# A linear-attention block with an MLP on one core: the state product with its values stationary, a query-state product in four row parts, fixed PSUM places, and a new order of work

## The chip, the core and the metric

The kernel runs on one core of a Trainium2 chip. A core has a matrix engine (TensorE, in the profile PE, its weight loads PEld), a vector engine (VectorE, DVE), a scalar engine (ScalarE, ACT), a general engine (GpSimd, POOL) and a sync engine (SyncE, SP) that issues most transfers. Each engine works through its own instructions in order and waits on semaphores for the others. Matmuls write into PSUM, which here is eight banks of 512 fp32 values per partition; everything else lies in SBUF.

The metric is the time of one execution on the device in microseconds (us), median of several runs. Lower is better.

## What is computed

The input is one sequence of 2048 tokens of 640 features. First comes an attention block without a softmax over tokens: each of 32 heads (20 features each) maps queries and keys through a small matrix, takes a softmax over its 20 features of the result and of its negative, and uses these 40 numbers as positive features. Keys and values are summed over all tokens into a state of 40 x 20 a head, and each query reads the state. Then comes an MLP of width 1728. Both have a layer norm in front and a residual around them.

```python
def _A_ref(x, wqkv, w_phi, wo):
    ...
    pq = jnp.einsum("bhsd,hdf->bhsf", q, w_phi)
    pk = jnp.einsum("bhsd,hdf->bhsf", k, w_phi)
    phi_q = jnp.concatenate([_softmax(pq, axis=-1), _softmax(-pq, axis=-1)], axis=-1)
    phi_k = jnp.concatenate([_softmax(pk, axis=-1), _softmax(-pk, axis=-1)], axis=-1)
    kv = jnp.einsum("bhsf,bhsd->bhfd", phi_k, v)
    z  = jnp.einsum("bhsf->bhf", phi_k)
    num = jnp.einsum("bhqf,bhfd->bhqd", phi_q, kv)
    den = jnp.einsum("bhqf,bhf->bhq", phi_q, z)[..., None] + 1e-6
    o = num / den
    return (...)(o, 0, 2, 1, 3).reshape(B, S, D) @ wo
...
h = x + _A_ref(_layernorm(x, axis=-1), A_wqkv, A_w_phi, A_wo)
h2 = h + _B_ref(_layernorm(h, axis=-1), B_w1, B_w2)
```

## The kernel before

The 2048 tokens are 16 token tiles of 128 (t = 0 to 15), in four groups of four. The 640 features are five chunks of 128 (c or r). All operations are small functions op_xx, and a long string, ORDER, names them one by one with their arguments; the kernel walks through it, so each engine's instructions stand in the order of the string. The last letter of a word chooses an engine (a ACT, v VectorE, p POOL) or a queue (s SP).

The stages, with the words that the text below uses:

- Weights and input are loaded (lp, lk, lv, lx for w_phi, the key weights, the value weights and X; l1, l2, lo later). wt turns a chunk of the key weights (five transposes), wc copies it out, fk folds w_phi into it and fc copies the folded chunk Wfk. gk and gc do the same for the queries (lq loads these weights turned).
- For each tile, st takes the statistics on VectorE, rs the inverse deviation on POOL, xn normalizes, and either xt and xc (TensorE transposes and a copy) or xd (a transposing DMA) turn the tile. At the start VectorE fills a tile of zeros, and TensorE runs matmuls on it (wm, L255).
- vp and kp project values and keys: ten matmuls of 320 columns each. vc copies the values to Vp (32 heads of 20 values and a one, 21 columns), ke takes the exponential of plus and minus the keys on ACT, kr sums each head on VectorE, and ka divides on POOL (one of the 16 tiles is shared with VectorE, kb).
- cc, the **state product** (L407), adds a tile to the state in PSUM: for each sign s and each of ten slices of 64 key features one matmul, with 64 keys' columns as weights and four heads of Vp as 84 moving columns. The output's 64 partitions are the upper or lower half, so two matmuls stand side by side on the two column halves of the array. km multiplies the state by a mask, so that only a head's own block is left, into KVBD (bf16).
- qp projects queries (matmuls of 512 columns, five for each chunk of 128 features), qe takes the exponentials into EqT, with the features on partitions.
- dp, the **query-state product** (L460), runs once for each tile and sign: ten matmuls over 64 partitions (row halves), each of 88 columns (four heads of 22). dw then joins both signs: a reciprocal, a product of 32 columns, a product and an add of 672 columns on VectorE (L473 to L480). dr takes one more reciprocal, do divides on POOL or VectorE, td turns the tile by a transposing DMA.
- op multiplies by wo (ten matmuls of 320 columns), oa adds X on VectorE, sq, sa, sr and hn are the second layer norm, hd turns the tile.
- up is the MLP's first product (L596, and L606 for the last 64 rows), ua the silu on ACT, yp the second product (L642, and yh, L657, for the last 64 rows), yo adds the residual, so stores a tile.

PSUM is one pool of four buffers of two banks each. Every op_ function that needs one takes the next that comes free; the running state holds one of them for the whole key stage. The product of one tile takes two, one for each sign.

Of the kernel before, what the change touches and what calls it, by code (L numbers as in the profile page):

```python
# [9 lines left out]
ALU = mybir.AluOpType  # L10
# [18 lines left out]
lq.4 wc.4.v fc.3.a st.1 mo xt.2 kp.3.0.1 lq.0 xc.2.a kp.3.1.2 kp.3.2.3 st.0 fk.4 vp.2.0.3 fc.4.a  # L29
lx.8.12.s rs.0.2 lq.3 vp.3.3.5 kp.3.3.4 vc.3.a kp.3.4.5 xn.0.v vp.2.3.5 lq.1 xn.1.v ke.3 st.5  # L30
kp.2.0.1 kp.2.1.2 xt.0 lh.s kp.2.2.3 st.4 xc.0.a kp.2.3.4 xt.1 vc.2.a kp.2.4.5 lq.2 kp.0 st.6 rs.4.2
ke.2 xn.5.v vp.0 xc.1.a xn.4.v xd.5 st.7 ke.0 kp.1 st.11 lx.12.16.s rs.6.2 vc.0.a xd.4 st.8 vp.1
ke.1 xn.7.v st.10 gk.2 xd.7 gk.0 gc.2.a vp.5 st.9 vc.1.a lo.s gc.0.a kr.1 gk.3 rs.8.4 kp.5 gc.3.a
rm.10 gk.1 xn.9.v ke.5 ka.1.p vp.4 st.12 xd.9 gc.1.a st.14 kp.4 vc.5.a xn.8.v vc.4.a rm.6 st.15 xd.8
vp.7 ke.4 st.13 kp.7 xn.6.a kr.2 rs.12.4 xn.10.a xd.6 vp.9 ke.7 rm.13 xn.12.v ka.2.p kr.4 kp.9 xd.12
vc.9.a vc.7.a gk.4 l2.0.4.s ke.9 vp.8 xd.10 xn.14.v ka.4.p kr.0 gc.4.a vp.6 xn.13.a vc.8.a kr.3 kp.6
rm.11 rm.15 ka.0.p cc.2 kr.7 cc.1 ke.6 cc.4 kp.8 ka.3.p vc.6.a kr.5 xn.15.a qp.0.0 ke.8 xd.15 ka.7.p
kr.9 xd.14 vp.12 qe.0.0 l2.8.13.s ka.5.p kr.8 kp.12 l1.1.s vc.12.a xn.11.a qp.1.0 ke.12 ka.8.p xd.11
kr.12 kp.15 l1.0.s qe.1.0 xd.13 ka.9.p kp.10 l1.2.s l2.4.8.s cc.0 cc.7 ka.12.p ke.10 cc.3 cc.5 cc.8
kr.10 vp.10 kp.14 vc.10.a kr.6 ka.10.p ke.15 kp.11 ke.14 kp.13 ka.6.h ke.11 kr.14 vp.15 ke.13 kr.11  # L40
ka.14.p qp.0.2 qp.0.1 qe.0.2 kr.13 vc.15.a ka.11.p vp.13 kr.15 vp.14 ka.13.p vc.13.a qe.0.1 kb.6
vp.11 vc.14.v ka.15.p cc.12 vc.11.a cc.9 cc.6 cc.11 cc.10 cc.14 cc.13 cc.15 qp.1.2 km.0 close km.1
dp.1.0 qe.1.2 dp.1.1 qp.1.1 dw.1.v dp.0.1 qe.1.1 dp.0.0 dr.1 qp.2.1 dw.0.v dp.3.1 qe.2.1 dp.3.0 dr.0
qp.3.0 dw.3.v do.0.0.p do.0.1.p do.1.1.p td.0 dp.5.0 qe.3.0 dp.5.1 dr.3 qp.2.0 dw.5.v do.3.1.p
do.3.0.p do.1.0.p dp.4.1 td.1 qe.2.0 dp.4.0 op.0 dw.4.v td.3 qp.2.2 oa.0 dp.2.1 qe.2.2 dp.2.0 dr.5
sa.0 qp.3.2 dr.4 dw.2.v do.5.1.p sq.0 op.1 do.5.0.p qe.3.2 sr.0 td.5 dp.9.0 dp.9.1 dr.2 qp.3.1 hn.0
do.2.1.p do.2.0.v hd.0 oa.1 do.4.0.p do.4.1.p dw.9.v sq.1 td.2 op.3 sa.1 qe.3.1 sr.1 td.4 op.5 hn.1
dr.9 hd.1 op.2 oa.5 oa.3 sa.5 op.4 do.9.1.p oa.2 up.0.3 sq.2 oa.4 dp.10.1 sa.4 sq.4 dp.10.0 up.0.0
dw.10.v ua.0.3 sr.4 sq.5 sa.3 do.9.0.p dp.6.0 ua.0.0 dp.6.1 up.0.1 sa.2 dw.6.v td.9 sq.3 sr.3 dp.8.1
dr.10 ua.0.1 dp.8.0 sr.2 up.0.2 dw.8.v sr.5 do.10.0.p dp.7.0 do.10.1.v ua.0.2 dp.7.1 op.9 dr.6 hn.5  # L50
do.6.1.p hn.3 hd.5 do.6.0.p hn.2 yp.0.0 hn.4 hd.2 oa.9 yp.0.1 dw.7.v td.6 hd.3 yp.1.0 dr.8 do.8.0.v
hd.4 yh.0.0 dp.11.0 dp.11.1 yo.0 yp.1.1 do.8.1.v dr.7 dw.11.v do.7.1.p op.6 sa.9 up.1.0 do.7.0.v
# [12 lines left out]
ua.4.2 up.3.2 ua.3.4 yp.15.0 ua.3.2 up.3.5 yp.14.0 ua.3.5 yp.15.1 yp.10.0 yh.4.0 yh.3.0 yp.12.1
yp.12.0 yp.14.1 yo.12 so.12 yp.10.1 yp.11.1 yo.10 yo.14 yp.11.0 so.14 so.10 yh.3.1 yo.15 yq.13.0
yo.11 so.15 so.11 so.9 yq.13.1 yz.13.0 yz.13.1 sz.13.0.a sz.13.1.s
# [3 lines left out]
def kernel(  # L71
# [11 lines left out]
    nc = tc.nc  # L83
# [18 lines left out]
    HQ = [(64 * q) // DH for q in range(2 * C)]  # L102
# [8 lines left out]
    mm = ctx.enter_context(tc.tile_pool(name="mm", bufs=4, space=PSUM))  # L111

    def mm2():
        return mm.tile([P, 2, 512], F32, name="mm2")

    def mmT():
        return mm.tile([P, C, P], BF16, name="mm2")
# [14 lines left out]
    warm = first.tile([P, 512], BF16, name="warm")  # L132
    nc.vector.memset(warm[:], 0.0)
# [8 lines left out]
    maskS = persist.tile([P, C, 4, 1], BF16, name="maskS")  # L142
    KVBD = persist.tile([P, 2, C, 4, 22], BF16, name="KVBD")
# [58 lines left out]
    def op_mc():  # L202
        nc.gpsimd.memset(maskS[:], 1.0)
        d = 64 - DH * HQ[1]
        for lo in (0, 64):
            m = maskS[lo : lo + 64, :, :, 0]
            nc.gpsimd.affine_select(
                out=m, in_=m, compare_op=ALU.is_ge, fill=0.0,
                base=0, pattern=[[d, C], [-DH, 4]], channel_multiplier=1,
            )  # L210
            nc.gpsimd.affine_select(
                out=m, in_=m, compare_op=ALU.is_gt, fill=0.0,
                base=DH, pattern=[[-d, C], [DH, 4]], channel_multiplier=-1,
            )
        for s in range(2):
            nc.gpsimd.tensor_copy(KVBD[:, s, :, :, 21], maskS[:, :, :, 0])

# [35 lines left out]
    def op_wm(n=512, ps=None):  # L253
        ps = mm2() if ps is None else ps
        nc.tensor.matmul(ps[:, 0, 0:n], warm[:, 0:P], warm[:, 0:n], start=True, stop=True)  # L255
        return ps
# [78 lines left out]
    def op_gc(ce, eng="a"):  # L335
        copy(
            eng,
            Wfq[:, ce, :].rearrange("p (r a k) -> p a r k", r=C, a=2),
            tl["gk", ce][:, :, 0:320].rearrange("p a (r k) -> p a r k", r=C),
        )  # L340
# [54 lines left out]
    def op_cc(t):  # L395
        Ek, Vp = tl["ek", t], Vps[t % NV]
        if "kv" not in tl:
            kv = mm2()
            tl["kv"] = [kv[:, s, 0:420].rearrange("p (r j c) -> p r j c", r=C, j=4) for s in range(2)]
            tl["nkv"] = 0  # L400
        kv = tl["kv"]
        tl["nkv"] += 1
        for s in range(2):
            for r in range(C):
                for a in range(2):
                    q, lo = C * a + r, 64 * a
                    nc.tensor.matmul(  # L407
                        kv[s][lo : lo + 64, r, :, :].rearrange("p j c -> p (j c)"),
                        Ek[:, s, 64 * q : 64 * q + 64],
                        Vp[:, HQ[q] : HQ[q] + 4, :].rearrange("p h c -> p (h c)"),  # L410
                        start=(tl["nkv"] == 1 and r == 0),
                        stop=(tl["nkv"] == T),
                        skip_group_check=True,
                    )

    def op_km(s):
        nc.vector.tensor_tensor(
            KVBD[:, s, :, :, 0:21], tl["kv"][s], maskS[:].to_broadcast([P, C, 4, 21]), op=ALU.mult,
        )
# [34 lines left out]
    def op_dp(t, s):  # L454
        g, i = t // GT, t % GT
        ps = mm2()
        for r in range(C):
            for a in range(2):
                lo = 64 * a
                nc.tensor.matmul(  # L460
# [26 lines left out]
    def op_dr(t):  # L487
        rd = sm.tile([P, 2, 16], F32, name="rd")
        nc.vector.reciprocal(rd[:], tl["u", t][:, :, :, 20])  # L489
        tl["rd", t] = rd  # L490
# [228 lines left out]
```

## Time and profile before

| | us |
|---|---|
| median of 3 runs | 239.62 |
| range of the runs | 239.39 to 239.97 |
| the profiled execution, its own time | 240.42 |
| its span (first to last instruction) | 238.7 |
| VectorE, ACT, POOL busy | 136.3, 104.8, 88.8 |

The profile is one execution. A view that groups instructions gives busy time and the mean time of one; as matmuls overlap, a mean holds the latency, and the time that a matmul really takes is the distance between starts. The chain of waits is followed back from the last instruction: each piece is what the end depended on. In the timeline, the first number of a row is the start in us from the span's start, the second the length; a bracket gives the idle time of the engine before it and who ended it.

### The profile page before, as it was taken

How to read it: one execution, taken by the hardware profiler on the slowest of the kernel's cores; microseconds unless marked ns; L12 is line 12 of the kernel's file. 1: busy time of each engine (PE TensorE's matmuls, PEld its weight loads, DVE VectorE, ACT ScalarE, POOL GpSimd, SP SyncE). 2: the span in 40 equal slices, each digit the busy share in tenths (PEclk: the TensorE clock that was granted, in tenths of full speed). 3: DMA queues.
4: the chain of work that ended last, by engine and by line, in shares of the span. 5: the costliest groups of instructions: out<-in, count | busy, mean ns of one | idle time of the engine just before them, and what ended most of it. 6: DMA issues, size and time to landing. Idle time of an engine off the chain costs nothing.

```text
span 238.7 us, 5187 instructions
## 1 busy us (share of the span) xinstructions
PE 232.9 (98%) x2143; PEld 150.8 (63%) x2159; DVE 136.3 (57%) x256; ACT 104.8 (44%) x155; POOL 88.8 (37%) x166
## 2 busy tenths in 40 slices
PE   7999999999999999999999999999999999999994
PEld 3777777577584456787655476664566756656762
DVE  3779999938968999889858139623213120000133
ACT  3678897967545674561043620015660014631000
POOL 5722769998870737464101550001424000000000
PEclk9999999999999999999999999999999999999999
DMA  6997945499000136116480004520103701000013
GB/s 204 314 212 168 233 89 140 87 333 312 4 3 3 27 58 110 31 29 58 84 133 7 17 14 82 110 58 0 29 3 83 156 11 55 0 3 0 26 59 110
DMA packets 42807, 20.60 MB, mean 86 GB/s; under 512 B 34336, under 2 KB 42272, under 8 KB 42784
## 3 DMA queue, kind: packets, MB, share of 16 engines
q1 hardware_dynamic: 41984, 20.11, 36.8%
q8 instruction: 17, 0.28, 0.5%
q10 hardware_dynamic: 800, 0.16, 0.4%
q14 instruction: 6, 0.05, 0.1%
HBM read 9.61 MB, written 2.62 MB: 51 GB/s over the span
## 4 chain that ended last, share of the span: by engine, by line
PE 93%; DVE 2%; DMA 2%; issue 1%; ACT 1%; DVEq 0%
PE mm L596 24%; PE mm L642 21%; PE mm L348 18%; PE mm L427 9%; PE mm L522 9%; PE mm L460 3%; PE mm L407 3%; DMA out_dram<-ob 2%; PE mm L255 2%; PE mm L318 1%; PE mm L606 1%; PE mm L657 1%; ACT EqT L437 1%; PE mm L303 1%; DVE xn L278 1%
## 5 line engine op out<-in xcount | busy, mean ns | idle before, releaser
L618 ACT ACTIVATE shT<-mm 128x1024 bf16<-128x1024 f32 (+2 forms) x29 | 27.5, 963 | 77.9 <-PE mm L596 56.2
L596 PE MATMUL mm<-HnT,w 128*128 128x512 bf16 (+1 forms) x316 | 58.7, 335 | 0.5
L642 PE MATMUL mm<-w,shT 128*128 128x320 bf16 (+2 forms) x415 | 58.5, 299 | 0.2 <-issue 0.2
L642 PEld LDWEIGHTS <-shT 128*128 128x128 bf16 x416 | 39.8, 98 | 17.8 <-issue 1.3
L596 PEld LDWEIGHTS <-w 128*128 128x128 bf16 x325 | 31.2, 98 | 23.1 <-issue 0.4
L665 DVE TENSOR_TENSOR ob<-mm,X 128x640 bf16<-128x640 f32 x15 | 12.2, 822 | 46.7 <-PE mm L642 38.3
L348 PEld LDWEIGHTS <-XnT 128*128 128x128 bf16 x320 | 30.8, 98 | 12.3 <-DMA wv<-in_A_wqkv_dram 0.2
L385 POOL TENSOR_TENSOR Ek<-Ek,Sk 128x1280 bf16<-128x1280 bf16 (+1 forms) x16 | 36.9, 2332 | 2.5 <-DVE Sk L380 1.6
L377 DVE TENSOR_REDUCE Sk<-Ek 128x64 f32<-128x1280 bf16 x16 | 23.1, 1445 | 4.5 <-ACT Ek L369 4.5
L437 ACT ACTIVATE EqT<-mm 128x1024 bf16<-128x1024 f32 (+1 forms) x24 | 19.8, 879 | 11.0 <-PE mm L427 11.0
L348 PE MATMUL mm<-Wfk,XnT 128*128 128x320 bf16 x160 | 24.2, 299 | 0.0
L348 PE MATMUL mm<-wv,XnT 128*128 128x320 bf16 x160 | 24.0, 299 | 0.1
L522 PE MATMUL mm<-wo,ot 128*128 128x320 bf16 x160 | 23.8, 299 | 0.0
L427 PE MATMUL mm<-XnT,Wfq 128*128 128x512 bf16 x94 | 23.1, 380 | 0.4
L495 POOL TENSOR_TENSOR o<-u,rd 128x320 bf16<-128x320 f32 x21 | 15.7, 768 | 20.4 <-DVE rd L489 12.0
L531 DVE SCALAR_TENSOR_TENSOR X<-mm,X 128x640 bf16<-128x640 f32 x16 | 12.9, 815 | 17.2 <-PE mm L522 17.2
L369 ACT ACTIVATE Ek<-mm 128x640 bf16<-128x640 f32 x32 | 20.6, 717 | 4.1 <-PE mm L407 3.0
L522 PEld LDWEIGHTS <-ot 128*128 128x128 bf16 x160 | 15.3, 98 | 7.4 <-issue 0.3
L544 POOL TENSOR_SCALAR HM<-HST 128x1 f32<-128x1 f32 x16 | 3.4, 210 | 40.0 <-DVE X L531 40.0
L427 PEld LDWEIGHTS <-Wfq 128*128 128x128 bf16 x100 | 9.2, 97 | 10.2 <-issue 0.3
L261 DVE BATCH_NORM_STATS2 stats<-X 128x6 f32<-128x320 bf16 x32 | 13.6, 467 | 2.7 <-DMA X<-in_A_x_dram 2.7
L561 DVE TENSOR_SCALAR hn<-X,HM 128x640 bf16<-128x640 bf16 x16 | 7.9, 525 | 12.2 <-POOL HM L555 12.2
(71 smaller groups left out, 212.8 us busy)
## 6 DMA issues: line engine op xcount, KB each, us to landing
out_dram<-ob SPq DMA_DIRECT2D x15, 160.0 KB, 2.0
w<-in_B_w_dram SPq DMA_DIRECT2D x3, 720.0 KB, 6.5
X<-in_A_x_dram SPq DMA_DIRECT2D x3, 640.0 KB, 4.9
w<-in_B_w_dram SPq DMA_DIRECT2D x2, 640.0 KB, 6.0
wk<-in_A_wqkv_dram SPq DMA_DIRECT2D x5, 160.0 KB, 3.4
wo<-in_A_wo_dram SPq DMA_DIRECT2D x1, 800.0 KB, 6.7
w<-in_B_w_dram SPq DMA_DIRECT2D x1, 800.0 KB, 5.3
wv<-in_A_wqkv_dram SPq DMA_DIRECT2D x1, 480.0 KB, 5.8
```

The lines of the kernel that those rows point to most:

```text
L261: nc.vector.bn_stats(stats[:, k, :], X[:, t, k * 320 : (k + 1) * 320])
L348: nc.tensor.matmul(ps[:, half, 0:320], tok(XnT[t // GT], t)[:, c, :], W[:, c, half * 320 : (half + 1) * 320], start=(c == 0), stop=(c == C ...
L369: nc.scalar.activation(Ek[:, s, :].rearrange("p (a n) -> p a n", a=2), tl["kp", t][:, :, 0:320], AF.Exp, scale=1.0 - 2.0 * s,)
L377: nc.vector.tensor_reduce(Sk[:], tl["ek", t][:].rearrange("p s (h f) -> p (s h) f", f=DH), axis=AX.X, op=ALU.add,)
L385: eng.tensor_tensor(Ek3, Ek3, tl["sk", t][:, lo:hi].unsqueeze(2).to_broadcast([P, hi - lo, DH]), op=ALU.mult,)
L427: nc.tensor.matmul(ps[:, k, :], Wfq[:, c, r * P : (r + 1) * P], XnT[g][:, c, :], start=(c == 0), stop=(c == C - 1),)
L437: nc.scalar.activation(E[:, s, rs[0] : rs[-1] + 1, :], tl["qp", g, i][:, 0 : len(rs), :], AF.Exp, scale=1.0 - 2.0 * s,)
L495: (nc.vector if eng == "v" else nc.gpsimd).tensor_tensor(tl["o", t][:, a * 320 : (a + 1) * 320].rearrange("p (h f) -> p h f", f=DH), tl["u ...
L522: nc.tensor.matmul(ps[:, half, 0:320], tl["ot", t][:, c, :], wo[:, c, half * 320 : (half + 1) * 320], start=(c == 0), stop=(c == C - 1),)
L596: nc.tensor.matmul(ps[:, i * W : (i + 1) * W], w1[:, c, fc * P : (fc + 1) * P], HnT[g][:, c, 0:W], start=(c == 0), stop=(c == C - 1), skip ...
L618: nc.scalar.activation(sh[:, a:b], tl["up", g, k][:, 0 : b - a], AF.Silu)
L642: nc.tensor.matmul(ps, shT[g][:, fc * W + i * P : fc * W + (i + 1) * P], w2[:, fc, a:b], start=first and fc == 0, stop=last and fc == FC - ...
```

## The change

The state product takes the values as weights: three heads of Vp, 63 columns, and 120 moving columns, the plus and minus keys of these three heads. There are eleven such products a tile (the last with two heads, 80 columns), alternating between the two column halves. The result is turned the wrong way round for what follows, so it is copied once, at the end, into a tile KVT (kt, by ACT and VectorE), and turned by 40 small matmuls against a pattern made of the identity (tk), whose outputs are 32 partitions each; km masks the result as before, now with three heads a part.

The query-state product runs once a tile for both signs, as 40 matmuls over 32 partitions each (row quarters) with 66 columns; each quarter writes into its own bank, so that a tile takes half of PSUM, four banks. PSUM is two fixed tiles of four banks (half0, half1), and a second string, PLACES, tells each user which two banks, or which half, it takes. dw, dr and do read the new layout. The warm-up matmuls read a constant of ones. The value weights come as chunk 1 to 2, 0, 3 to 4. gc copies in two parts. ORDER is a new one.

```diff
-    mm = ctx.enter_context(tc.tile_pool(name="mm", bufs=4, space=PSUM))
+    mm = ctx.enter_context(tc.tile_pool(name="mm", bufs=1, space=PSUM))
+    half = [mm.tile([P, 4, 512], F32, name=f"half{i}") for i in range(2)]
+    place = iter(PLACES.replace("\n", ""))
     def mm2():
-        return mm.tile([P, 2, 512], F32, name="mm2")
+        k = int(next(place))
+        return half[k // 2][:, k % 2 * 2 : k % 2 * 2 + 2, :]
+    def mm4():
+        return half[int(next(place)) // 2]
...
-    warm = first.tile([P, 512], BF16, name="warm")
-    nc.vector.memset(warm[:], 0.0)
+    warm = nc.const_aps.tensor(1.0, [P, 512], BF16)
...
+    def op_mz(eng):
+        e = nc.vector if eng == "v" else nc.gpsimd
+        e.memset(KVT[:], 0.0)
+        e.tensor_tensor(
+            rot[:].rearrange("p (x n) -> p x n", x=2),
+            ident[:, 0:63].unsqueeze(1).to_broadcast([P, 2, 63]),
+            ident[:, 64:127].unsqueeze(1).to_broadcast([P, 2, 63]), op=ALU.add,
+        )
...
     def op_cc(t):
...
-        for s in range(2):
-            for r in range(C):
-                for a in range(2):
-                    q, lo = C * a + r, 64 * a
-                    nc.tensor.matmul(
-                        kv[s][lo : lo + 64, r, :, :].rearrange("p j c -> p (j c)"),
-                        Ek[:, s, 64 * q : 64 * q + 64],
-                        Vp[:, HQ[q] : HQ[q] + 4, :].rearrange("p h c -> p (h c)"),
...
+        for G in range(NG):
+            n = min(3, H - 3 * G)
+            lo, b, k = FH * (G % 2), G // 2 // 3, G // 2 % 3
+            nc.tensor.matmul(
+                tl["kv"][lo : lo + 21 * n, b, 120 * k : 120 * k + 40 * n].rearrange("p (s f) -> p s f", s=2),
+                Vp[:, 3 * G : 3 * G + n, :].rearrange("p h c -> p (h c)"),
+                Ek[:, :, 60 * G : 60 * G + 20 * n],
...
+    def op_kt(a, eng):
+        lo, kv = FH * a, tl["kv"]
+        for b, n in ((0, 3), (1, 2)):
+            copy(
+                eng,
+                KVT[lo : lo + 63, :, 360 * b : 360 * b + 120 * n].rearrange(
+                    "p s (j x f) -> p x j s f", x=2, f=60)[:, a],
+                kv[lo : lo + 63, b, 0 : 120 * n].rearrange("p (j s f) -> p j s f", s=2, f=60),
+            )
+        if a == 0:
+            copy(eng, KVT[0:42, :, 600:640], kv[0:42, 1, 240:320].rearrange("p (s f) -> p s f", s=2))
+
+    def op_tk():
+        ps = mm2()
+        tl["kv2"] = [ps[:, s, 0:315].rearrange("p (r j c) -> p r j c", r=C, j=3) for s in range(2)]
+        for s in range(2):
+            for r in range(C):
+                for g in range(4):
+                    lo, q, h = 32 * g, 160 * g + 32 * r, 8 * g + HW[r]
+                    nc.tensor.matmul(
+                        tl["kv2"][s][lo : lo + 32, r, :, :].rearrange("p j c -> p (j c)"),
+                        KVT[:, s, q : q + 32], rot[:, h % 3 * 21 : h % 3 * 21 + 63],
+                        start=(r == 0), stop=(r == C - 1), skip_group_check=True,
+                    )
...
-    def op_dp(t, s):
-        g, i = t // GT, t % GT
-        ps = mm2()
-        for r in range(C):
-            for a in range(2):
-                lo = 64 * a
-                nc.tensor.matmul(
-                    ps[:, a, HQ[r] * 22 : (HQ[r] + 4) * 22],
-                    EqT[g][lo : lo + 64, s, r, i * P : (i + 1) * P],
-                    KVBD[lo : lo + 64, s, r, :, :].rearrange("p j c -> p (j c)"),
...
+    def op_dp(t):
+        G, i = t // GT, t % GT
+        ps = mm4()
+        for s in range(2):
+            for r in range(C):
+                for g in range(4):
+                    lo, o = 32 * g, 176 * s + 22 * HW[r]
+                    nc.tensor.matmul(
+                        ps[:, g, o : o + 66],
+                        EqT[G][lo : lo + 32, s, r, i * P : (i + 1) * P],
+                        KVBD[lo : lo + 32, s, r, :, :].rearrange("p j c -> p (j c)"),
...
     def op_dw(t, eng="v"):
         A = tl["dp", t]
-        w = sm.tile([P, 2, 16], F32, name="w")
+        w = sm.tile([P, 4, 8], F32, name="w")
         nc.vector.reciprocal(w[:], A[1][:, :, :, 21])
         nc.vector.tensor_tensor(w[:], w[:], A[0][:, :, :, 21], op=ALU.mult)
...
         nc.vector.tensor_tensor(
-            u[:], A[1][:, :, :, 0:21], w[:].unsqueeze(3).to_broadcast([P, 2, 16, 21]), op=ALU.mult,
-        )
...
+            u[:], A[1][:, :, :, 0:21], w[:].unsqueeze(3).to_broadcast([P, 4, 8, 21]), op=ALU.mult,
+        )
+        nc.vector.tensor_tensor(u[:], u[:], A[0][:, :, :, 0:21], op=ALU.add)
```

The orders around the start and around the turn of the state, before and after (words of other engines stand among TensorE's; "..." marks words left out):

```diff
-lp.a lx.2.4.s ta lk.2.3.s lk.0.1.s mk lk.3.4.s lk.1.2.s lk.4.5.s lv.0.3.s ph.p lx.1.2.s st.3
-lx.0.1.s wt.2 lv.3.5.s st.2 wc.2.a rs.3 lx.4.8.s wm.512 wt.0 wm.256 wt.3 wc.0.a fk.2 wc.3.v rs.2
-wt.1 fc.2.a fk.0 xn.3.v fk.3 wc.1.v mc fc.0.a xt.3 fk.1 xc.3.v wt.4 fc.1.a xn.2.v wm.256 vp.3.0.3
+lp.a lx.2.4.s ta lk.1.2.s lk.2.3.s mk lk.0.1.s lx.1.2.s lk.3.4.s lx.0.1.s lk.4.5.s st.2 ph.p
+lx.4.8.s lv.1.3.s wm.256.3 wt.1 st.3 lv.0.1.s wt.2 wc.1.a rs.2 lx.8.12.s wt.0 wc.2.v fk.1 lv.3.5.s
+wc.0.a rs.3 xn.2.v lx.12.16.s st.1 fc.1.a xt.2 wt.3 fk.0 xc.2.a wc.3.v fk.2 fc.0.a xn.3.v fk.3 st.0
+fc.2.a xt.3 kp.2.0.1 kp.2.1.2 xc.3.a wt.4 rs.0.2 kp.2.2.3 fc.3.a wc.4.v kp.3.0.1 kp.3.1.2 fk.4 mz.p
...
-vp.11 vc.14.v ka.15.p cc.12 vc.11.a cc.9 cc.6 cc.11 cc.10 cc.14 cc.13 cc.15 qp.1.2 km.0 close km.1
-dp.1.0 qe.1.2 dp.1.1 qp.1.1 dw.1.v dp.0.1 qe.1.1 dp.0.0 dr.1 qp.2.1 dw.0.v dp.3.1 qe.2.1 dp.3.0 dr.0
+qp.2.2 qe.0.0 ka.15.p cc.6 cc.13 cc.9 qe.0.1 cc.11 cc.8 cc.12 cc.15 cc.14 qp.0.2 kt.1.a kt.0.v close
+tk qe.0.2 qp.1.2 km.1 km.0 qe.2.2 dp.0 qe.1.2 dw.0.v qp.1.0 qe.1.0 dp.3 qp.2.0 dw.3.v dr.0 qe.2.0
+dp.1 dr.3 qp.1.1 dw.1.v do.3.0.p do.3.1.p do.0.0.p do.0.1.v qe.1.1 dp.2 qp.2.1 td.0 dw.2.v td.3 dr.1
+qe.2.1 dp.5 dr.2 do.1.1.p op.0 dw.5.v ...
```

In PLACES, which has a digit a user (0 and 1 the two pairs of banks of half0, 2 and 3 those of half1), tiles 0, 3, 1, 2 and 5 of the query-state product stand in half0 and the query projections between them in half1; tiles 4, 9 and 10 follow in half1.

More of the change, by code (lines that the diff above doesn't have):

```diff
@@ L101 @@
     NH = [(128 * r + 127) // DH - HLO[r] + 1 for r in range(C)]
-    HQ = [(64 * q) // DH for q in range(2 * C)]
+    HW = [0, 1, 3, 4, 5]
+    NG = 11
     x_t = A_x.rearrange("b (p t) d -> p (b t) d", p=P)
@@ L251, in op_ta, with op_wm @@
         nc.scalar.activation(ones4[:, 1:2], nhalf[:, 1:2], AF.Exp)
[L253 to L256, printed above, removed]
+    def op_wm(n=512, k=3):
+        nc.tensor.matmul(half[k // 2][:, k % 2 * 2, 0:n], warm[:, 0:P], warm[:, 0:n], start=True, stop=True)
     def op_st(t):
@@ L335, in op_gc @@
     def op_gc(ce, eng="a"):
[L336 to L339, printed above, removed]
-        )
+        for a in range(2):
+            copy(
+                eng,
+                Wfq[:, ce, :].rearrange("p (r a b k) -> p a b r k", r=C, a=2, b=2)[:, a],
+                tl["gk", ce][:, a, 0:320].rearrange("p (b r k) -> p b r k", b=2, r=C),
+            )
     def proj(key, t, W, lo, hi):
@@ L397, in op_cc @@
         if "kv" not in tl:
[L398 to L401, printed above, removed]
+            tl["kv"], tl["nkv"] = mm2(), 0
         tl["nkv"] += 1
+        for G in range(NG):
[5 more added lines that the diff above has]
+                Ek[:, :, 60 * G : 60 * G + 20 * n],
+                start=(tl["nkv"] == 1 and k == 0),
+                stop=(tl["nkv"] == T),
+                skip_group_check=True,
+            )
```

135 lines of the change are left out of this document (66 added, 69 removed).

## The prediction

> **What bounds the kernel now.** I read the page first, then the chain of waits in order of time, then the list of waits, then short stretches of the timeline around the places that the diff touches.
>
> ```profile
> span 238.7 us, 5187 instructions
> PE 232.9 (98%) x2143; PEld 150.8 (63%) x2159; DVE 136.3 (57%) x256; ACT 104.8 (44%) x155; POOL 88.8 (37%) x166
> PE   7999999999999999999999999999999999999994
> PE 93%; DVE 2%; DMA 2%; issue 1%; ACT 1%; DVEq 0%
> ```
>
> TensorE is full in every slice but the first and the last, and it carries 93% of the chain. The list of waits has only three entries for TensorE, none behind 11.1 us. So a TensorE instruction saved is time saved, as long as nothing new makes TensorE wait, and each new wait is paid in full. What one matmul really takes is read from runs of equal ones in the chain; the means in the group list (some 200 to 380 ns) hold the latency too.
>
> ```profile
> 46.69 2.16 PE mm L427 x10
> 48.85 2.72 PE mm L348 x20
> 67.80 3.23 PE mm L407 x152
> 12.46 0.32 PE mm L318 x6
> ```
>
> 512 columns take 216 ns, 320 take 136 ns: 0.417 ns a column and 2.5 ns on top. That gives 37.5 ns for 84 columns, 39.2 for 88, 52.5 for 120, 30.0 for 66, 28.8 for 63, 35.8 for 80. Of the third row's run 160 matmuls belong to it (some records are missing): 20.2 ns each, half of 37.5 and some: the two column halves run side by side.
>
> ```profile
> L407 PE MATMUL mm<-Vp,Ek x320: 198/200/225, 39.0 to 70.8; 128*64 128x84 bf16 x160
> L460 PE MATMUL mm<-KVBD,EqT x320: 199/202/210, 72.1 to 150.2; 64*128 64x88 bf16 x160
> ...
> 71.84 0.38 PE L427 MATMUL mm<-XnT,Wfq 128*128 128x512 bf16 x1
> 72.15 0.57 PE L460 MATMUL mm<-KVBD,EqT 64*128 64x88 bf16 x20
> 72.64 0.39 PE L427 MATMUL mm<-XnT,Wfq 128*128 128x512 bf16 x1
> 72.75 0.36 DVE L473 RECIPROCAL w<-mm 128x32 f32<-128x32 f32 x1 [0.58 <-PE mm L460]
> ```
>
> One query-state block (L460): ten pairs at 39.2 ns make 0.39 us, and the next full matmul begins 0.49 us after the block does: 0.10 us is lost going back to full tiles. Going in, 72.15 - 71.84 is 0.31 where 0.216 was due: 0.095. **A change of tile shape costs 0.095 us.**
>
> **The change, part by part, on TensorE.** (a) State product: 20 matmuls of 84 columns a token tile, in pairs 10 x 37.5 = 0.375 us; now 11, of which the lower column half has six (five of 120 columns, one of 80): 5 x 52.5 + 35.8 = 0.298. Sixteen tiles: -1.2 us. Bounds: no loss if the halves run side by side as now; if a 63 column load broke this, 11 matmuls one by one, 0.56 a tile, +3.0. I take the first, since L407's loads are as small and pair.
> (b) The turn (tk), 40 matmuls of 63 columns on four 32-column parts: ten fours of 28.8 ns, 0.29 us; one after the other at L407's 20.2 ns, 0.81. I take 0.29.
> (c) Query-state product: 40 matmuls of 66 columns in four row parts, each part in its own bank: ten fours of 30.0 ns against ten pairs of 39.2, so 16 x 0.092 = -1.5 us. The other end is in the rivals.
> (d) Tile shapes: blocks of the state product, of this product and of the MLP remain; tk adds two changes, and since row parts of 32 no longer share a shape with the half tiles (L657) that stood beside blocks, three more come by the order of the matmuls. 5 x 0.095 = +0.5.
> Sum on TensorE: -1.9 us.
>
> The page "TensorE: Matmul & The Clock Gate" of the Trainium skill says in its section "Wait — 56ns, not 53.3ns?" that start to start of matmuls never falls below about 25 ns, however few the columns. That speaks against (c): 40 x 25 would be 1.0 us a tile instead of 0.30, and the estimate from that page some 250 us. The trace disagrees: L407 has 20.2 ns, changes of shape included.
>
> **Startup.**
>
> ```profile
> L348 PE MATMUL mm<-Wfk,XnT 128*128 128x320 bf16 x20 | 3.5, 299 | 0.0
> L348 PE MATMUL mm<-wv,XnT 128*128 128x320 bf16 x20 | 3.2, 298 | 0.1
> L303 PE MATMUL mm<-ident,wk 128*128 128x128 bf16 x25 | 3.1, 275 | 0.0
> L318 PE MATMUL mm<-phb,wTk 128*128 128x140 bf16 (+1 forms) x30 | 2.3, 221 | 0.0
> L289 PE MATMUL mm<-ident,xn 128*128 128x128 bf16 x20 | 1.8, 219 | 0.5 <-DVE xn L278 0.5
> ...
> 1.24 3.59 PE mm L255 x8
> 4.84 0.58 PE mm L303 x5
> 9.18 1.87 DVE xn L278
> 11.04 0.05 issue
> 11.09 0.45 PE mm L289 x5
> ```
>
> These groups are those up to 16.86 us; two of the 40 L348 belong behind that, so the work done by then is 38 x 0.136 + 45 x 0.056 + 30 x 0.053 = 9.3 us, and 7.6 are lost: warm-up matmuls (L255) until the first weight chunk lands near 4.7, slow first matmuls, and near 10.5 a wait for VectorE's second normalized tile (xn). The new order sends X's tiles 0 and 1 ahead of the fourth weight chunk, and the value weights behind X; it normalizes tiles 2 and 3 before it turns to statistics, and starts with key projections. I walked it by hand: weight turns from 4.9, xt.2 at 7.4, xt.3 at 9.4 (xn.3 waits for the statistics of tile 1), first key projection at 9.7, the third finished near 14.9. By then 8.2 us of work are done, 6.7 lost. Gain 0.8; bounds +0.3 (a landing a little late) and -1.6. The value weights, as two DMAs now, go out behind 640 KB of X, but are first read after 14.9. TensorE no longer waits for VectorE's fill of the warm tile; the ninth and tenth warm matmul fill that time, so I count nothing.
>
> **What comes late behind the saving.** TensorE's state product ends as POOL's last normalization does:
>
> ```profile
> 33.45 4.79 POOL L385 TENSOR_TENSOR Ek<-Ek,Sk 128x1280 bf16<-128x1280 bf16 x2 [0.21 <-DVE Sk L380]
> 60.53 9.88 POOL L385 TENSOR_TENSOR Ek<-Ek,Sk 128x1280 bf16<-128x1280 bf16 x4 [1.13 <-DVE Sk L380]
> ```
>
> The new order ends VectorE's statistics earlier, so POOL's second one starts near 30.5; fourteen more at 2.35 us end near 65, and the last products then ask for them at 65.5. Room of half a microsecond: no cost, 1 us if POOL slips. POOL's new fills and mask steps lie ahead of its first normalization, where it idles.
>
> Next the turn itself:
>
> ```profile
> 65.71 1.95 ACT L437 ACTIVATE EqT<-mm 128x1024 bf16<-128x1024 f32 x2
> 67.84 0.69 ACT L163 CAST Vp<-mm 128x640 bf16<-128x640 f32 x1 [0.18 <-PE mm L348]
> 68.11 0.81 DVE L161 CAST Vp<-mm 128x640 bf16<-128x640 f32 x1
> 71.08 1.10 DVE L417 TENSOR_TENSOR KVBD<-mm,maskS 128x420 bf16<-128x420 f32 x2 [2.15 <-PE mm L407]
> ```
>
> The state is copied by ACT (600 columns, some 0.7 us by its 640 column row) and VectorE (680 columns in three, 0.9), while TensorE has five matmuls of 216 ns. ACT's copy is queued behind two query exponentials, 3.9 us, and TensorE gives it only 1.1 + 0.1 + 2.4 + 1.1 us after their first input is ready: tk starts 0.2 us late (bounds 0 and 0.8). The masking after it (315 columns, 0.83 us by proportion, at most 1.10) lies under five more matmuls and just fits.
>
> Then the query-state tiles, where I expect most of what is given back:
>
> ```profile
> 74.54 0.85 DVE L480 TENSOR_TENSOR u<-u,mm 128x672 f32<-128x672 f32 x1
> 74.91 0.57 PE L460 MATMUL mm<-KVBD,EqT 64*128 64x88 bf16 x20
> ...
> 99.21 0.36 DVE L473 RECIPROCAL w<-mm 128x32 f32<-128x32 f32 x1 [0.42 <-PE mm L460]
> 99.67 0.19 DVE L474 TENSOR_TENSOR w<-w,mm 128x32 f32<-128x32 f32 x1
> 99.90 0.86 DVE L476 TENSOR_TENSOR u<-mm,w 128x672 f32<-128x672 f32 x1
> 100.79 0.85 DVE L480 TENSOR_TENSOR u<-u,mm 128x672 f32<-128x672 f32 x1
> ```
>
> Before, the second tile's product starts at 74.91, ahead of the end of VectorE's add at 75.39: each of its two parts takes whichever of four buffers is free. Now one tile holds a fixed half of PSUM, both signs mixed in every bank, and tiles 0, 3, 1, 2, 5 all stand in the same half: each waits for the last add of the one before. From a block's first matmul to the next one's: 0.27 (nine steps of 30 ns) + 0.24 (the last matmul's 0.20 and 0.03 to the reciprocal, 72.75) + 2.43 (99.21 to 101.64) + 0.05 (as between 11.04 and 11.09) = 2.99. TensorE's own work in between is 0.30 + 0.19 + 2.16 = 2.65. Each loses 0.34: tiles 1, 2, 5 and, in the other half, 10 make 1.35, tile 3 some 0.1, since qp.1.0 ahead of it is late itself. Bounds 0 and 2.3, with op.4 and tile 4 waiting for VectorE and qp.1.0 for ACT. I take 1.45.
>
> **Sum:** -1.9 - 0.8 + 0.2 + 1.45 = -1.05 us, say -1.0. The profiled execution took 240.42 us, its span 238.7; after, 239.4 and 237.7. The median of the runs shown is 0.8 below that execution, 239.62, so I forecast **238.6 us**.
>
> **Rivals.** *No new waits*: VectorE has room (57% over the span), and the saving stays whole: 238.6 - 1.65 = 237.0. For it: no waits before, with the same VectorE work; against: the bank wait above, in an order fixed by the file. *Only two of four row parts run at once*: then a four takes 60.0 ns, a block 0.60 instead of 0.30, 16 x 0.30 = +4.8, the turn +0.3: 243.7, slower. For it: the trace shows only pairs, and one matmul after another at 20.2 ns would give 0.81 a block and, with a turn of 0.81, 247 (0.03 of this rival's chance); against: within a pair nothing queues, as 39.2 ns is what one matmul alone takes. It decides above 30.0 + 1.0/160 = 36 ns a four. *A side engine is late elsewhere* (POOL's chain before the turn, or a landing in startup, 1 us): 239.6. For it: POOL's margin; against: POOL idles over 1 us at 60.5 already.
>
> **How the numbers follow.** About 0.2%, 0.5 us, is what a measurement here can tell from no change. Forecast 0.43 (its own range 237.6 to 239.6), no waits 0.2, two row parts 0.17, side engine 0.2. Faster: 0.43 x 0.85 + 0.2 + 0.2 x 0.2 = 0.6; slower: 0.17 + 0.2 x 0.4 + 0.02 = 0.27; the same 0.13. The range, 236.4 to 241.2, holds all but the row part case and takes in the bounds of startup and stalls.
>
> **What would show it.** In the changed kernel's lines: the state product (L425) at 0.30 us a tile; a query-state block (L504) with its next full matmul 0.40 us after its start (0.70 would be the second rival); in the list of waits L504 behind VectorE's add (L524) some 0.34 us four times (none: the first rival); the turn (L453) once behind a copy; no wait for POOL at L425; the third key tile finished by 15. A block over 0.47, or waits over 3 us in all, would make the prediction wrong.

## The result, and the profile after

The changed kernel takes 303.94 us (median of 5 runs, 302.35 to 304.47) beside 239.62 before: a ratio of 1.2669, 95% interval 1.2627 to 1.2711. The prediction was 238.6.

Three lines of the page of the changed kernel, to be read beside those of before (span; busy time and share of each engine; TensorE's busy tenths in 40 slices):

```profile
span 302.1 us, 5659 instructions
PE 241.0 (80%) x2374; PEld 150.3 (50%) x2374; DVE 131.6 (44%) x254; ACT 109.0 (36%) x165; POOL 92.9 (31%) x180
PE   7868977768886578588778877986879898887995
```

No engine works more than 5% longer than before. TensorE is idle for 302.1 - 241.0 = 61 us where it was idle for 5.8, and the holes are spread over the whole span: only 6 of the 40 slices have a 9. So this isn't one late transfer or one slow stage but something that every stage has. The list of waits of the changed kernel (waiting engine, tile and line, what it waited for: us in total, times, longest) names it:

```profile
PE half L636 <- ACT shT L658: 9.7, 10, 1.6
PE half L370 <- ACT Ek L391: 6.1, 6, 1.4
PE half L470 <- ACT EqT L480: 5.8, 5, 1.6
PE half L562 <- ACT EqT L480: 4.5, 2, 2.9
...
PE half L425 <- ACT Ek L391: 1.8, 1, 1.8
```

Each row is a matmul that waits for a copy out of PSUM, and none of them reads what that copy makes: the output projection (L562) doesn't read the query exponentials (EqT), and the state product (L425) reads Ek as POOL or VectorE leaves it and not as ACT's exponential (L391) does. Such a wait can be for the last reader of the same two banks, or for a reader of the other two banks of the same half. PLACES tells which. L562 and L425 are of the second kind: the output projection of tile 0, for one, writes into the second pair of `half1` and waits for the exponential that reads the first pair. What waiter and releaser share there is only a name, `half0` or `half1`. TensorE's list of before has no row that names a copy out of PSUM.

The chain of waits, in order of time, shows what this does (start, length, what), here in the MLP's first product:

```profile
208.73 6.65 PE half L636 x30
...
215.41 1.03 ACT shT L658
...
216.48 2.33 PE half L636 x10
...
218.84 1.03 ACT shT L658
...
219.91 1.24 PE half L636 x5
```

By ORDER and PLACES, the last ten of the matmuls that end at 215.38 fill the second pair of `half1`, those at 216.48 the first pair, and those at 219.91 the second again. The copy at 218.84 reads the second pair. It has been full since 215.38, but the copy starts only when TensorE has filled the first pair too; and TensorE then waits for this copy, as the second pair is the next that it needs. So a copy waits for matmuls into the other pair, and a matmul for copies. They no longer overlap here, though PSUM has eight banks, and each turn costs the copy's 1.03 us and some 0.07 to change over.

The theory: the waits that are built into the program go by named PSUM tile. With four tiles of two banks, a matmul waits for the last reader of its own two banks, and a copy for the last matmul into them. With two tiles of four, each waits for the last access to any of the four, so the two users that stand in one half at a time take turns.

### The profile page after: what moved, and what is told of

It is laid out like the page before. It is cut to its first block, busy times and chain, and to the rows that moved or that the text cites. A ratio compares the mean times of both kernels' runs of the same rounds, so it can differ in the third digit from the quotient of the medians.

```text
span 302.1 us, 5659 instructions
## 1 busy us (share of the span) xinstructions
PE 241.0 (80%) x2374; PEld 150.3 (50%) x2374; DVE 131.6 (44%) x254; ACT 109.0 (36%) x165; POOL 92.9 (31%) x180
## 5 line engine op out<-in xcount | busy, mean ns | idle before, releaser
L636 PE MATMUL half<-HnT,w 128*128 128x512 bf16 (+1 forms) x325 | 59.5, 336 | 14.0 <-ACT shT L658 9.7
L682 PE MATMUL half<-w,shT 128*128 128x320 bf16 (+2 forms) x416 | 58.7, 299 | 5.8 <-ACT shT L658 3.3
L658 ACT ACTIVATE shT<-half 128x1024 bf16<-128x1024 f32 (+2 forms) x29 | 27.6, 965 | 85.8 <-PE half L636 61.8
L682 PEld LDWEIGHTS <-shT 128*128 128x128 bf16 x416 | 39.8, 98 | 24.3 <-issue 8.0
L407 POOL TENSOR_TENSOR Ek<-Ek,Sk 128x1280 bf16<-128x1280 bf16 (+1 forms) x16 | 36.6, 2309 | 15.7 <-DVE Sk L402 15.7
L562 PE MATMUL half<-wo,ot 128*128 128x320 bf16 x160 | 25.3, 313 | 9.5 <-ACT EqT L480 4.5
L470 PE MATMUL half<-XnT,Wfq 128*128 128x512 bf16 x100 | 23.4, 379 | 7.2 <-ACT EqT L480 5.8
L370 PE MATMUL half<-Wfk,XnT 128*128 128x320 bf16 x160 | 24.8, 299 | 5.3 <-ACT Vp L176 2.6
L370 PE MATMUL half<-wv,XnT 128*128 128x320 bf16 x160 | 23.8, 299 | 6.1 <-ACT Ek L391 5.0
L480 ACT ACTIVATE EqT<-half 128x1024 bf16<-128x1024 f32 (+1 forms) x24 | 19.6, 884 | 19.1 <-PE half L470 17.6
L571 DVE SCALAR_TENSOR_TENSOR X<-half,X 128x640 bf16<-128x640 f32 x16 | 12.9, 819 | 29.7 <-PE half L562 13.2
L562 PEld LDWEIGHTS <-ot 128*128 128x128 bf16 x160 | 16.3, 102 | 17.1 <-issue 10.2
L391 ACT ACTIVATE Ek<-half 128x640 bf16<-128x640 f32 x32 | 20.2, 715 | 5.3 <-PE half L370 4.7
L176 ACT CAST Vp<-half 128x640 bf16<-128x640 f32 x16 | 10.9, 696 | 14.9 <-PE half L370 13.4
```

The costliest lines, as they stand in the source:

```text
L370: nc.tensor.matmul(ps[:, half, 0:320], tok(XnT[t // GT], t)[:, c, :], W[:, c, half * 320 : (half + 1) * 320], start=(c == 0), stop=(c == C ...
L391: nc.scalar.activation(Ek[:, s, :].rearrange("p (a n) -> p a n", a=2), tl["kp", t][:, :, 0:320], AF.Exp, scale=1.0 - 2.0 * s,)
L407: eng.tensor_tensor(Ek3, Ek3, tl["sk", t][:, lo:hi].unsqueeze(2).to_broadcast([P, hi - lo, DH]), op=ALU.mult,)
L470: nc.tensor.matmul(ps[:, k, :], Wfq[:, c, r * P : (r + 1) * P], XnT[g][:, c, :], start=(c == 0), stop=(c == C - 1),)
L480: nc.scalar.activation(E[:, s, rs[0] : rs[-1] + 1, :], tl["qp", g, i][:, 0 : len(rs), :], AF.Exp, scale=1.0 - 2.0 * s,)
L562: nc.tensor.matmul(ps[:, half, 0:320], tl["ot", t][:, c, :], wo[:, c, half * 320 : (half + 1) * 320], start=(c == 0), stop=(c == C - 1),)
```

## The experiments

**Four tiles instead of two.** Everything as in the changed kernel, its places too, but PSUM as four tiles of two banks.

```diff
-    half = [mm.tile([P, 4, 512], F32, name=f"half{i}") for i in range(2)]
+    pair = [mm.tile([P, 2, 512], F32, name=f"pair{i}") for i in range(4)]
...
-                        ps[:, g, o : o + 66],
+                        ps[g // 2][:, g % 2, o : o + 66],
...
-        nc.vector.reciprocal(w[:], A[1][:, :, :, 21])
+        for x in range(2):
+            nc.vector.reciprocal(w[:, 2 * x : 2 * x + 2], A[1][x][:, :, :, 21])
```

> PSUM as four tiles of two banks instead of two of four; the query-state product writes into two of them, and the joining of the signs (reciprocal, two products, add) runs as two instructions over half the columns each. Everything else is the changed kernel. Theory (each instruction waits for the last reader of its whole PSUM tile, so four-bank tiles make TensorE wait for the copy of the neighbouring pair): the 64 us go, the time is 236 to 243 us, TensorE waits for ACT and VectorE less than 6 us in all. Rival 1 (the new order, or the state product and its turn, leave TensorE waiting): above 290 us. Rival 2 (the small row-part matmuls are the cost): above 290 us too.

246.08 us (244.33 to 246.41) beside 239.91: ratio 1.0254, 1.0228 to 1.0280. Of 64 us, 58 are gone, though the time lies above the 236 to 243 that was expected. Two lines of its page, and all of TensorE's waits that its list now has:

```profile
span 242.6 us, 5716 instructions
PE 232.7 (96%) x2355; PEld 148.7 (61%) x2374; DVE 134.8 (56%) x318; ACT 108.4 (45%) x165; POOL 92.8 (38%) x180
...
PE pair L567 <- DMA ot<-o: 2.0, 2, 1.1
PE pair L310 <- DVE xn L299: 1.1, 2, 0.6
PE pair L277 <- PEq L747: 0.8, 1, 0.8
PE pair L370 <- DMA XnT<-xn: 0.8, 1, 0.8
PE pair L425 <- POOL Ek L407: 0.6, 1, 0.6
PE pair L504 <- DVE u L529: 0.2, 1, 0.2
PE pair L453 <- DVE KVT L174: 0.2, 1, 0.2
```

No wait for a copy out of the other pair is left. What is left is 5.7 us of waits: 0.8 at TensorE's own start, 0.2 for VectorE's last read of a query-state product, the rest for inputs that come late. The list of before has 1.9.

**The tiles alone.** The kernel before, with its own products and its own order; only its PSUM buffers are given, at the banks that they had, as slices of two four-bank tiles. The control gives the same banks as slices of four two-bank tiles.

```diff
     def mm2():
-        return mm.tile([P, 2, 512], F32, name="mm2")
+        k = int(next(place))
+        return half[k // 2][:, k % 2 * 2 : k % 2 * 2 + 2, :]
```

> The kernel before, with its own order and products, only its PSUM buffers laid into two tiles of four banks, each user at the very banks that it had. Theory: TensorE waits for the neighbour's copy, the time rises by 30 us or more, to 270 to 320. Rivals 1 and 2: nothing changes, 239.6 us.

> Control for the run beside it: the same fixed places, as four tiles of two banks. All theories: 239 to 241 us; a theory that fixed places as such cost time would have it above 245.

304.9 us and 240.7, one run each, beside 239.91. The page of the first, and two rows of its list of waits; then the busy line of the control:

```profile
span 303.2 us, 5200 instructions
PE 244.7 (81%) x2143; PEld 153.7 (51%) x2159; DVE 135.8 (45%) x256; ACT 105.3 (35%) x155; POOL 88.3 (29%) x166
...
PE half L356 <- ACT Ek L377: 4.3, 4, 1.7
...
PE half L650 <- DVE u L484: 4.2, 3, 1.7
```

```profile
PE 231.9 (97%) x2143; PEld 149.8 (63%) x2159; DVE 134.9 (56%) x256; ACT 104.8 (44%) x155; POOL 88.9 (37%) x166
```

The same matmuls on the same banks: 65 us from the naming alone, and 0.8 from fixing the places, which is within the range of before's own runs (239.77 to 240.85). The MLP's second product (L650) waiting for the attention's sum (u) is the same kind of row as above. This settles the main cause: neither the new products nor the new order is needed for the loss.

**The products without the tiles and without the order.** The pool and the order of before; the state product with values stationary, its turn, and the query-state product in four row parts (in two buffers, so that its four VectorE steps are two instructions each). POOL's fill for the turn (`mz`) comes with it.

```diff
-cc.13 cc.15 qp.1.2 km.0 close km.1 dp.1.0 qe.1.2 dp.1.1
+cc.13 cc.15 qp.1.2 kt.1.a kt.0.v close tk qp.2.2 qe.1.2 km.0 km.1 qe.2.2 dp.1.0 dp.1.1
...
-        ps = mm2()
+        ps = [mm2(), mm2()]
```

> The kernel before, with its pool of four free buffers and its order, and only the two products changed: values stationary with the copy and the turn (one block of five query matmuls moved up behind the turn), and the query-state product in four row parts, written into two buffers, signs joined per buffer. Theory (the sizes of the prediction on TensorE hold, and what was lost came from PSUM tiles and the new order): -1.2 -1.5 +0.3 +0.5, up to 0.8 for the turn's wait: 237.7 to 238.5 us. Rival (VectorE's chain sets the pace of the query tiles, TensorE's saving turns into waiting): 239.3 to 240.5 us.

244.23 us (243.66 to 244.31) beside 239.39: ratio 1.0181, 1.0145 to 1.0217. Both theories missed, the gain isn't there. Four of the larger rows of its list of waits:

```profile
PE mm L262 <- DVE xn L251: 1.0, 1, 1.0
PE mm L596 <- DVE ob L665: 0.9, 1, 0.9
...
PE mm L522 <- DVE X L531: 0.7, 1, 0.7
...
PE mm L377 <- POOL Ek L359: 0.5, 1, 0.5
```

It is a collection, each row with another releaser; all rows come to 6.5 us, for 1.9 before, and the spans differ by 3.8 (242.5 and 238.7). Where the query-state product stands, 74.8 to 95 us, the windows of before and then of this kernel show which engine is full (stretch: its length, then busy us and instructions of PE, PEld, DVE, ACT, POOL, the granted clock, DMA share and GB/s):

```profile
74.80:95.00 20.20, 19.98 (x208) 10.90 (x211) 18.81 (x39) 13.18 (x18) 10.68 (x21) 1.00 0.30 54
```

```profile
74.80:95.00 20.20, 18.81 (x319) 9.64 (x319) 19.17 (x65) 10.67 (x15) 9.68 (x18) 1.00 0.32 43
```

Before, TensorE had 0.2 us of room and VectorE 1.4; now VectorE has 1.0 and TensorE 1.4. The query-state product became cheaper on TensorE, and VectorE is now the fuller of the two. Ahead of that, POOL's normalizations end at 70.4 us as before, so what the state product saves is waited for there (the Ek row). The starts of the query-state blocks show where the time goes: the seventh is 1.2 us behind before's (90.77 and 89.53), the eighth 2.7 (101.46 and 98.80), with output projections between them that wait for VectorE (the X row), the last 2.6 (152.49 and 149.87), and the ob row lies behind that. So VectorE's pace is a part of the 4.8 us and not the whole.

**The state product in another way.** As the last, but keys stationary in blocks of 32 columns on four column parts: 40 matmuls of 63 columns a tile, and no turn.

```diff
-        for G in range(NG):
-            ...
+        for s in range(2):
+            for r in range(C):
+                for g in range(4):
+                    ...
+                        Ek[:, s, q : q + 32],
+                        Vp[:, h : h + 3, :].rearrange("p h c -> p (h c)"),
```

> As the run beside it, but the state product is not turned round: the keys stay stationary, 32 columns at a time on four column parts, 63 moving columns, 40 matmuls a tile, straight into the layout that the four row parts need; no copy and no turn. Theory (four parts run at once at 28.8 ns a four): 0.29 us a tile against 0.375, so -1.4 -1.5 +0.3: 236.8 to 237.6 us. Rival (many small matmuls in a row are held at some 20 ns each): 0.8 us a tile, 245 us or more.

246.53 us (246.24 to 247.73): ratio 1.0299, 1.0250 to 1.0347. It lies in the rival's range, but not by the rival's mechanism. The timeline of TensorE around the end of the state product (start, length, engine, line; in brackets the idle time before and what ended it):

```profile
66.98 1.78 PE L410 MATMUL mm<-Vp,Ek 128*32 128x63 bf16 x195
70.91 1.19 PE L410 MATMUL mm<-Vp,Ek 128*32 128x63 bf16 x125 [2.14 <-issue]
72.03 0.82 PE L430 MATMUL mm<-XnT,Wfq 128*128 128x512 bf16 x3
74.64 0.59 PE L430 MATMUL mm<-XnT,Wfq 128*128 128x512 bf16 x2 [1.78 <-issue]
```

195 matmuls go by in 1.78 us, 9 ns each; then TensorE stands for 2.1 us and soon again for 1.8, and no engine and no transfer of the kernel's data releases it. What the DMA queues did from 68 to 73 us (mean busy share in 40 slices, then the one queue that moved anything: packets, MB, share):

```profile
DMA  0000400000000000000000000000000500000000
q8 instruction: 2, 0.03, 2.5%
```

Two transfers of instructions start there, near 68.5 and 71.9 us, each ahead of a gap, and TensorE goes on 2.4 to 2.7 us after each.

**The same, spread.** The last eight tiles of the state product aren't in one block any more, but between projections.

```diff
-cc.12 vc.11.a cc.9 cc.6 cc.11 cc.10 cc.14 cc.13 cc.15 qp.1.2
+qp.0.2 cc.12 ... cc.9 ... vp.13 kr.15 cc.10 vp.14 ... vp.11 ... cc.6 cc.11 qp.0.1 qe.0.1 cc.13 cc.14 cc.15 qp.1.2
```

> The four_column_parts kernel (246.53 us) with the state product's last eight tiles no longer in one block: tiles 12, 9 and 10 stand between value and query projections, tiles 6 and 11 ahead of one query projection, tiles 13, 14, 15 behind it. Theory: the gaps of 2.1 and 1.8 us that its list of waits puts down to 'issue' come from TensorE running through its own instructions (two for each small matmul, 640 in a row) faster than they are fetched; 195 matmuls went by in 1.78 us ahead of the first gap. With 80 to 120 in a row at most, broken by five matmuls of 216 ns or ten of 136 ns, both gaps go: 3.5 to 3.9 us less, 242.6 to 243.2, and no issue row over 0.5 us for TensorE. Rival: the time is lost per small matmul, or in what stands ahead of the turn to big ones, whatever the order: the same two gaps, 245.5 to 247.

243.47 us (243.31 to 243.97) beside 239.61: ratio 1.0170, 1.0152 to 1.0188; 3.1 us less than the block, and just above the range expected. The timeline of the same place:

```profile
67.54 0.66 PE L369 MATMUL mm<-Vp,Ek 128*32 128x63 bf16 x60 [0.87 <-DVE Ek L347]
...
70.39 1.16 PE L369 MATMUL mm<-Vp,Ek 128*32 128x63 bf16 x120
71.48 1.25 PE L389 MATMUL mm<-XnT,Wfq 128*128 128x512 bf16 x4
72.67 0.49 PE L426 MATMUL mm<-KVBD,EqT 32*128 32x66 bf16 x40
73.09 2.33 PE L389 MATMUL mm<-XnT,Wfq 128*128 128x512 bf16 x9
```

Both gaps are gone, for a wait of 0.87 for VectorE's share of tile 6 that the new order made. That the block of 320 makes the gaps is shown. It isn't the count alone: earlier, from 50.8 us on, both kernels run 200 such matmuls in a row without a gap. That TensorE outruns the fetching of its instructions fits the two transfers, but no run varied that alone, so it stays argued.

**Less work for VectorE.** The same with half of tile 2's division on POOL (`do.2.0.v` becomes `do.2.0.p`).

> As column_parts_spread, and half 0 of tile 2's division goes from VectorE to POOL. Theory: from the first query-state tile on VectorE is what TensorE waits for (0.30, 0.52 and 0.48 us between 87 and 97 in four_column_parts), so 1.0 us less on VectorE at 93.6 gives 0.4 to 0.9 back: 241.8 to 242.8. Rival: POOL's later division of tile 2 makes the transposing DMA late and the output projection waits for it instead: the same time as column_parts_spread or more.

243.66 us (243.11 to 244.06) for 243.47: no gain; the rival holds. TensorE's two waits for VectorE near 92 and 94 us are gone, and the output projection of tile 4 waits for its transposing transfer instead: POOL has the two halves of tile 2 to divide first.

```profile
98.58 1.53 PE L489 MATMUL mm<-wo,ot 128*128 128x320 bf16 x10 [1.38 <-DMA ot<-o]
```

**POOL's fills later.** The kernel with the new products in the old order, but with POOL's mask and fill work (`mc mz.p`) behind `rs.8.4`, and the same division on POOL.

> The old_order_new_products kernel (244.23 us) with two moves: POOL's mask and fill work for the new layout (from 7.7 to 12.9 us) goes behind the statistics of tiles 8 to 11, and half 0 of tile 2's division from VectorE to POOL. Theory: of the 7.7 us of gaps of over 0.2 us that TensorE had there, the one of 1.18 at 14.5 goes (0.7 to 1.1) and of those at 90.4, 93.4 and 95.7 another 0.4 to 0.9; the sum of the gaps is the whole loss, so the time falls with them to 242.2 to 243.1. Rival: TensorE's time is paced by POOL's normalizations up to 70 us and by VectorE behind it, so what the start gains is waited for again at 70: 243.3 to 244.3.

245.78 us (245.69 to 247.31): ratio 1.0277, 1.0245 to 1.0309, 1.5 us more than the order that it was to mend. Both theories missed. Two rows of its timeline:

```profile
7.64 1.51 POOL L163 MEMSET Vp<- 128x32 bf16 x10
...
34.28 1.73 ACT L256 ACTIVATE xn<-X,RS 128x640 bf16<-128x640 bf16 x2 [2.50 <-POOL RS L243]
```

The fill of Vp moved up to 7.64 with nothing ahead of it, beside a VectorE normalization that took 1.83 us instead of 0.44, and TensorE waits 1.1 us for that one; and at the new place of the mask work ACT waits 2.5 us for POOL's statistics, and TensorE 1.4 us for the exponential that is queued behind ACT's normalization.

**One fill out of the way.** The kernel before with the fill of Vp ahead of POOL's first product, where POOL waits for a transfer.

```diff
-... lv.0.3.s ph.p lx.1.2.s st.3
+... lv.0.3.s mo ph.p lx.1.2.s st.3
```

> The kernel before with one word moved: POOL's fill of the ones in the ten value tiles (1.56 us from 9.30) goes ahead of its first product, into the 1.79 us in which it waits for the transfer of w_phi. Theory: a VectorE normalization takes 0.44 us, but 1.86 where it runs beside this fill (9.18 in the profile of before, 7.50 in old_order_late_fills, none in old_order_new_products, whose fill lies beside no normalization); the 0.6 us that TensorE waits for the second normalized tile at 10.3 come from that. With the fill at 2.6 us all four normalizations take 0.44 and that wait goes: 0.4 to 0.9 us less, 238.7 to 239.2, ratio 0.996 to 0.998. Rival: TensorE waits there for the next thing (a copy of a folded chunk, or a transfer) as long: ratio 0.999 to 1.001.

239.60 us (239.09 to 240.02, 12 runs) beside 239.63: ratio 0.9992, 0.9976 to 1.0008. The rival holds. The normalizations up to 17 us, of before and then of this kernel, and the wait that took the place:

```profile
L278 DVE TENSOR_SCALAR xn<-X,MV,RS x4: 438/443/1858, 7.6 to 15.0; 128x640 bf16<-128x640 bf16 x4
```

```profile
L278 DVE TENSOR_SCALAR xn<-X,MV,RS x5: 437/445/447, 6.9 to 17.0; 128x640 bf16<-128x640 bf16 x5
...
PE mm L348 <- DMA wv<-in_A_wqkv_dram: 0.6, 1, 0.6
```

The slow normalization (shortest, middle and longest in ns) is cured, and with it the 0.5 us that TensorE waited for it in before's list (the expectation says 0.6). But TensorE waits no less: the value weights land no sooner. No version here beats the kernel before.

## Why the prediction was wrong

The step that failed is the one under "What comes late behind the saving": "Now one tile holds a fixed half of PSUM, both signs mixed in every bank, and tiles 0, 3, 1, 2, 5 all stand in the same half: each waits for the last add of the one before." The rule in it is right: who takes a tile waits for its last user. But it was applied to five query-state tiles (0.34 us for four of them, 0.1 for one), when the diff puts every user of PSUM into these two tiles. Of the other users the prediction named three, op.4, tile 4 and qp.1.0, in an upper bound of 2.3 us, and counted the rest at nothing. The cover that they took away, TensorE filling one pair of banks while ACT or VectorE empties the other, was never named. The trace of before had its price, ACT's copy in the MLP's first product:

```profile
L618 ACT ACTIVATE shT<-mm 128x1024 bf16<-128x1024 f32 x24 | 24.3, 1021 | 59.7 <-PE mm L596 56.2 <-PE mm L642 3.5
L369 ACT ACTIVATE Ek<-mm 128x640 bf16<-128x640 f32 x32 | 20.6, 717 | 4.1 <-PE mm L407 3.0 <-PE mm L348 1.0
```

24.3 us in the MLP alone, 20.6 and 19.8 more for the key and query exponentials, and TensorE's list of before waits for none of it: an estimate from these rows would have been tens of us. The tiles alone measured 65; that the three add up to 64.7 is chance, as TensorE's new waits are for VectorE's readers too. None of the rivals had it either.

The prediction named its own refutation, "waits over 3 us in all"; TensorE is idle for 61. The other steps, from the timeline of the changed kernel (state product) and then of the one with four tiles (turn, and two query-state tiles):

```profile
63.81 0.20 PE L425 MATMUL half<-Ek,Vp 128*42 128x80 bf16 x1
...
83.89 2.58 PE L425 MATMUL half<-Ek,Vp 128*63 128x120 bf16 x88
```

```profile
70.04 0.99 DVE L174 CAST KVT<-pair 63x360 bf16<-63x360 f32 x3 [5.36 <-ACT KVT L176]
...
70.62 0.84 PE L453 MATMUL pair<-rot,KVT 128*32 128x63 bf16 x40 [0.17 <-DVE KVT L174]
...
74.83 0.91 DVE L529 TENSOR_TENSOR u<-u,pair 128x336 f32<-128x336 f32 x2
...
75.38 0.20 PE L504 MATMUL pair<-KVBD,EqT 32*128 32x66 bf16 x2
...
75.80 0.49 PE L504 MATMUL pair<-KVBD,EqT 32*128 32x66 bf16 x38 [0.21 <-DVE u L529]
```

- (a) State product: eight tiles in 2.58 us less the last matmul's own 0.20 are 0.298 a tile, as predicted.
- (c) Query-state product: 40 matmuls in 0.49 us (72.67 in the spread kernel), of which some 0.19 are the last one's (L504's mean is 189 ns), so 0.30: four row parts run at once, and the rival with two falls. That is 7.5 ns a matmul; the 25 ns that "TensorE: Matmul & The Clock Gate" of the Trainium skill gives in its section "Wait — 56ns, not 53.3ns?" as the least from start to start don't hold here, as the prediction took it. The next full matmul comes 0.42 us after the block's start (72.67 to 73.09), for 0.40; with 0.49 before, a tile saves 0.07 us where 0.09 were counted, 1.1 in sixteen and not 1.5.
- (b), (d) The turn takes 0.77 us from its first matmul to the next projection (70.62 to 71.39), for 0.29 and a change of shape of 0.095. Two waits for the copies of the state are the reason, and the prediction had one of 0.2: 0.17 ahead of the turn, and 0.3 behind its second matmul. Both are for VectorE's copies, which start only when ACT's have ended (70.00 and 70.04); the prediction counted the two side by side. Both write into the one tile KVT, so this too fits waits that go by tile, but no run tested it.
- Startup: in the kernel with four tiles the third key tile ends near 15.7, not 14.9 (TensorE waits 1.1 us for xn there); in the changed kernel just 20 of the 30 matmuls had run by 16.86. The split value weights cost nothing, as costed: no row of waits names them.
- The query-state product's wait for VectorE's last step: predicted 1.45 us. In the changed kernel the list has 0.5, as TensorE waits elsewhere first. With four tiles the list has 0.2, but most of the wait is hidden, as the end of the matmul before (0.2 us) counts as busy: the blocks of tiles 3, 1, 2, 5 and 10 take 0.91, 0.62, 0.62, 0.70 and 0.74 us instead of 0.49, 1.1 more in all, and in each TensorE goes on 0.05 us after the add of the tile before has ended (75.74 and 75.80 for tile 3). So this step, mechanism and size, came out nearly as predicted.
- POOL's last normalization, predicted near 65 us and in time: with four tiles it ends at 68.45, and TensorE waits 0.6 us for it. The rival of a side engine had such waits, at 1 us in all.

So the saving would not have come even with four tiles. There the profiled span is 242.6 us for 238.7, and TensorE is busy for 232.7 us, for 232.9 before: of the 1.2 us of the state product the turn takes back 0.77, and the 1.1 of the query-state product are lost again in the five long blocks. On top come 5.7 us of listed waits, for 1.9 before. The medians lie 6.2 apart, 2 us more than these two profiled executions, and nothing here says where in a slower execution they lie. Nor was it tried to plan an order anew for the cheaper products.

## What to carry to other kernels

When buffers are merged into a bigger named tile, look up what every user of the tile then waits for, not only the one that needed the size: the cover that is lost is the copy out of one part under the filling of the other. A list of waits whose rows pair a reader and a writer that share no data shows this at once, and so does a copy that starts long after its banks are full. And in a kernel whose side engines have little room, price a TensorE saving only up to the place where POOL or VectorE sets the pace. A wait shorter than the latency of a matmul doesn't show as idle time: compare the lengths of equal blocks.

## What the hardware showed beside this

- A VectorE normalization of 128 x 640 bf16 takes 0.44 us, and 1.83 to 1.86 where POOL's ten small fills (1.5 us in all) run beside it; moving the fills alone cured it. "SBUF — State Buffer" in the Trainium skill says in its section "SBUF: two separate sides" that VectorE and GpSimd share a port pair which, for some of their instructions, the one that starts first holds to its end while the other blocks. The trace agrees that VectorE is held up, but for all ten fills and not for one, and though its own row starts first (9.18 for 9.30); the fills take as long as alone (1.56 us, and 1.52 where they were moved).
- After 195 small matmuls in 1.78 us TensorE stood still for 2.1 us with nothing of the kernel's to wait for; with that block of 320 broken up there was no such gap, and 200 in a row at an earlier place had none either.
